# Attention and MoE on one NeuronCore: the first two half sequences attended before any MoE product, reciprocals of those two spread by TensorE, weights loaded in eighths

## The chip, the cores and the metric

The kernel runs on one core of a Trainium2 chip. The metric is the device time of one execution in microseconds (us). A run that lies over 1.5% above the fastest of its kernel counts as slow and stays out of every ratio; the fast runs of one kernel spread over up to 1.5%. Medians and ranges in this text are over all runs of a kernel, the slow ones included. The profile is taken on one execution, and its span is that execution alone.

Engines in the profile: PE is the TensorE matmul, PEld its weight load, DVE VectorE, ACT ScalarE, POOL GpSimd, SP the engine whose queue issues most DMAs. The changed kernel calls its engines through a helper, so that all its lines show one line number (L62); there one reads by tile names. The granted clock is the share of full TensorE speed that the profile records. I call TensorE cold where its matmuls take up to twice as long as the same ones later, and warm otherwise.

## The reference, cut to what matters

Four sequences of 768 tokens, 8 heads of 64. Heads 0, 2 and 6 see everything before them ("retrieval"), the other five see 4 sink keys and a window of 64. The result goes through an MoE-shaped pair of products with a swish between:

```python
scores = scale * np.matmul(q, k.transpose(0, 1, 3, 2))
# ... causal mask for retrieval heads, causal & (sink | window) for the others
a = np.exp(scores)                       # after subtracting the maximum
a = a / (np.sum(a, axis=-1, keepdims=True) + 1e-09)
x = np.matmul(a, v)                      # -> (3072, 512) after putting heads side by side
h = x @ w_in                             # (512, 2048)
g = h * (1.0 / (1.0 + np.exp(-beta * h)))
return g @ w_out                         # (2048, 512)
```

## The kernel before

The work is cut into eight units: half a sequence of 384 queries each. Units 0 and 1 are the two halves of the first sequence. For a unit: load q and k, cast to bf16, transpose on TensorE ("QK"), copies of k for the window blocks ("KX"), scores, exponentials on ACT ("es"), masks on DVE, sums of the exponentials by matmuls, a reciprocal on DVE ("rec"), value products, and a normalizing multiply by the spread reciprocals ("R") that makes xT. Then 16 groups of four first products with w_in (h, tanh on ACT, gT on DVE), and 48 second products with w_out.

The sums of 8 heads stand on 8 partitions for each of 3 blocks of queries, but xT needs each of them on 64 partitions. The kernel writes them to DRAM and reads them back with a broadcast:

```python
        rec = rp.tile([96, 128], F32, name="rec")
        nc.vector.reciprocal(rec, sm[0:96, 0:128])
        rd = dp.tile([8, TU, 128], F32, name="rd")
        for j in range(TU):
            nc.sync.dma_start(out=rd[:, j, :], in_=rec[32 * j:32 * j + 8, :])
        R = rp.tile([128, NP, NQ], F32, name="R")
        src = rd[:]
        for i in range(2):
            nc.sync.dma_start(out=R[i * D:(i + 1) * D], in_=bass.AP(src.tensor, ...))
        # ... in pv(), after the value products of two pairs of heads:
        nc.vector.tensor_mul(x.xT[:, p0:p0 + 2, :], o[:, :, 0:NQ], x.R[:, p0:p0 + 2, :])
```

The identity for the transposes is made in f32 on POOL and cast on DVE, the weights come in quarters, and the order of everything follows from one loop: unit 0's attention, then in each step a piece of the next unit's attention, one first-product group of this unit, and three second products of the last unit.

```python
    ident_f = consts.tile([128, 128], F32, name="ident_f")
    make_identity(nc, ident_f)
    ident = consts.tile([128, 128], BF16, name="ident")
    nc.vector.tensor_copy(out=ident, in_=ident_f)
    # ...
    FS = d_ff // 4
    def load_w_in(s):
        # ... three DMAs for a quarter
        cast(nc.vector, w_in_sb[:, :, s * FS:(s + 1) * FS], f)
    # ...
    for s, f in pieces_a(0):        # the whole attention of unit 0
        f()
    for s in range(4):
        load_w_in(s)
    for s, f in pieces_l(1):        # loads of unit 1
        f()
    for s in range(4):
        load_w_out(s)
    for n in range(N + 1):
        lists = [pieces_a(n + 1), pieces_l(n + 2)]
        for s in range(FO):
            for l in lists:
                for st, f in l:
                    if st == s:
                        f()
            if n < N:
                mm1(units[n], s)
            if n > 0:
                mm2(units[n - 1], s, n == N)
```

The softmax here doesn't subtract the row's maximum and nothing guards it: scores larger than these inputs give would overflow.

Of the kernel before, what the change touches and what calls it, by code (L numbers as in the profile page):

```python
# [15 lines left out]

# [3 lines left out]
SH = [1, 3, 4, 5, 7]  # L20
# [14 lines left out]
def _aff(nc, buf, cm, fstep, base, n):  # L35
    nc.gpsimd.affine_select(
        out=buf,
        in_=buf,
        compare_op=GE,
        fill=0.0,  # L40
        base=base,
        pattern=[[fstep, n]],
        channel_multiplier=cm,
    )


def _view(ap, offset, dims):

    return bass.AP(ap.tensor, ap.offset + offset, [list(ap.ap[0])] + dims)
# [3 lines left out]
def kernel(  # L53
# [13 lines left out]
    nc = tc.nc  # L67
    B, H, S, D = q.shape
    T = S // 128
# [7 lines left out]
    def pool(name, bufs, space=None):  # L77
        kw = {} if space is None else {"space": space}
        return ctx.enter_context(tc.tile_pool(name=name, bufs=bufs, **kw))

    consts = pool("consts", 1)
    stg = pool("stg", 2)
    inp = pool("inp", 2)
    kxp = pool("kxp", 1)
    vp = pool("vp", 2)
    esp = pool("esp", 1)
    xp = pool("xp", 2)
    gp = pool("gp", 2)
    tp_ = pool("tanh", 3)
    op_ = pool("osb", 3)  # L90
    rp = pool("rec", 2)
    dp = pool("dram", 2, bass.MemoryType.DRAM)
    ps_s = pool("ps_s", 2, PSUM)
    ps_m = pool("ps_m", 1, PSUM)
    ps_h = pool("ps_h", 2, PSUM)
    ps_o = pool("ps_o", 1, PSUM)


    def cast(eng, dst, src):
        if eng is nc.scalar:  # L100
            nc.scalar.copy(out=dst, in_=src)
        else:
            eng.tensor_copy(out=dst, in_=src)  # L103

    qk_in = {}
    v_r = {}
    v_s = {}

    def load_qk(b, u, pi):
        ha, hb = PAIRS[pi]  # L110
        res = []
        for nm, src in (("q2", q), ("k2", k)):
            f = stg.tile([128, 2, TU, D], F32, name=nm + "f", bufs=4)
            eng = nc.scalar if (b, u, nm) == (0, 0, "k2") else nc.sync
            eng.dma_start(
                out=f,
                in_=bass.AP(src.tensor, src.offset + ((b * H + ha) * S + u * NQ) * D,
                            [[TU * D, 128], [(hb - ha) * S * D, 2], [1, TU * D]]),
            )
            c = inp.tile([128, TU, 2, D], BF16, name=nm)  # L120
            cast(nc.gpsimd if b > 0 and nm == "q2" else nc.vector, c.rearrange("p t a d -> p a t d"), f)
            res.append(c)
        qk_in[b, u, pi] = res

    def load_v(b, u):

        first_unit = (b, u) == (0, 0)

        def first():
            if u == 0:  # L130
                v_r[b] = vp.tile([128, 3, T, D], BF16, name="vr")
            v_s[b, u] = vp.tile([128, 5, NB[1], D], BF16, name="vs")

        def head(h):
            retr = RETR[h]
            i = (RH if retr else SH).index(h)
            key, step, nb = (u * NQ, 128, TU) if retr else (START[u], STEP[u], NB[u])
            f = stg.tile([128, NB[1], D], F32, name="vf", bufs=8)
            eng = nc.scalar if first_unit and h % 2 else nc.sync
            eng.dma_start(  # L140
                out=f[:, 0:nb, :],
                in_=bass.AP(v.tensor, v.offset + ((b * H + h) * S + key) * D, [[D, 128], [step * D, nb], [1, D]]))
            cast(nc.gpsimd, v_r[b][:, i, u * TU:(u + 1) * TU, :] if retr else v_s[b, u][:, i, 0:nb, :], f[:, 0:nb, :])

        def sinks():
            sk = stg.tile([SINK, H, D], F32, name="sk")
            nc.sync.dma_start(out=sk, in_=v[b, :, 0:SINK, :].rearrange("h p d -> p h d"))
            w0 = 1 if u == 0 else 0
            for i0, n, h, st in ((0, 2, 1, 2), (2, 2, 4, 1), (4, 1, 7, 1)):
                cast(nc.gpsimd, v_s[b, u][0:SINK, i0:i0 + n, w0:NB[u], :],  # L150
                     sk[:, h:h + (n - 1) * st + 1:st, :].unsqueeze(2).to_broadcast([SINK, n, NB[u] - w0, D]))

        return [first] + [lambda h=h: head(h) for h in RH + SH] + [sinks]

    for pi in range(NP):
        load_qk(0, 0, pi)
    for f in load_v(0, 0):
        f()


    ident_f = consts.tile([128, 128], F32, name="ident_f")
    make_identity(nc, ident_f)
    ident = consts.tile([128, 128], BF16, name="ident")
    nc.vector.tensor_copy(out=ident, in_=ident_f)  # L164
    m_f = consts.tile([128, 128], F32, name="m_f")
    nc.gpsimd.memset(m_f, 1.0)
    _aff(nc, m_f, -1, 1, 0, 128)
    mask_c = consts.tile([128, 128], BF16, name="mask_c")
    nc.vector.tensor_copy(out=mask_c, in_=m_f)

    s0_f = consts.tile([128, 128], F32, name="s0_f")
    nc.gpsimd.memset(s0_f, 1.0)
    _aff(nc, s0_f, 1, -1, W - 1, 128)
    nc.gpsimd.memset(s0_f[0:SINK, :], 1.0)
    _aff(nc, s0_f, -1, 1, 0, 128)
    sb_f = consts.tile([128, 60], F32, name="sb_f")
    nc.gpsimd.memset(sb_f, 1.0)
    _aff(nc, sb_f, 1, -1, -(SINK + 1), 60)
    _aff(nc, sb_f, -1, 1, W + SINK, 60)
    nc.gpsimd.memset(sb_f[0:SINK, :], 1.0)  # L180
    mask_s = []
    for u in range(2):
        m = consts.tile([128, NQ], BF16, name=f"mask_s{u}")
        for (blk, off, n) in BLOCKS[u]:
            src = s0_f if (u, blk) == (0, 0) else sb_f
            nc.gpsimd.tensor_copy(out=m[:, off:off + n], in_=src[:, 0:n])
        mask_s.append(m)


    esel = consts.tile([128, 8, 4, 8], BF16, name="esel")  # L190
    nc.gpsimd.memset(esel, 0.0)
    for j in range(8):
        nc.gpsimd.memset(esel[:, j, :, j:j + 1], 1.0)


    QK = []
    for pi in range(NP):
        t = consts.tile([128, 2, S], BF16, name=f"QK{pi}")
        nc.gpsimd.memset(t[:, 1, NQ:NQ + 128], 0.0)
        QK.append(t)  # L200

    beta_h = consts.tile([128, FO], F32, name="beta_h")
    nc.scalar.dma_start(out=beta_h, in_=moe_beta.rearrange("(fo fi) -> fi fo", fi=128))
    nc.vector.tensor_scalar(out=beta_h, in0=beta_h, scalar1=0.5, scalar2=None, op0=MULT)


    w_in_sb = consts.tile([128, NP, d_ff], BF16, name="w_in_sb")
    w_out_sb = consts.tile([128, FO, d_model], BF16, name="w_out_sb")
    FS = d_ff // 4

    def load_w_in(s):
        f = stg.tile([128, 4, FS], F32, name="wf")

        def rows(h, parts, step):
            return bass.AP(moe_w_in.tensor, moe_w_in.offset + h * D * d_ff + s * FS,
                           [[d_ff, parts], [step * D * d_ff, 2], [1, FS]])
        nc.sync.dma_start(out=f[0:D, 0:2, :], in_=rows(0, D, 1))
        nc.sync.dma_start(out=f[D:128, 0:2, :], in_=rows(2, D, 1))
        nc.sync.dma_start(out=f[:, 2:4, :], in_=rows(4, 128, 2))
        cast(nc.vector, w_in_sb[:, :, s * FS:(s + 1) * FS], f)  # L220

    def load_w_out(s):
        f = stg.tile([128, 4, FS], F32, name="wf")
        nc.sync.dma_start(out=f, in_=moe_w_out[s * 512:(s + 1) * 512, :].rearrange("(fo fi) d -> fi fo d", fi=128))
        cast(nc.gpsimd, w_out_sb[:, s * 4:(s + 1) * 4, :], f)


    KXs = {}

    def transpose_pair(x, pi):  # L230
        b, u = x.b, x.u
        c2 = qk_in.pop((b, u, pi))
        if (b, u) == (0, 0):
            ps = ps_h.tile([128, 2, TU, 128], BF16, name="h")
        else:
            ps = ps_m.tile([128, 2, TU, 128], BF16, name="misc")
        for i, c in enumerate(c2):
            for t in range(TU):
                nc.tensor.transpose(ps[:, i, t, :], c[:, t, :, :].rearrange("p a d -> p (a d)"), ident)  # L239
        nc.vector.tensor_copy(  # L240
            out=QK[pi][:, :, u * NQ:(u + 1) * NQ].rearrange("d a (p t) -> d a p t", t=TU),
            in_=ps.rearrange("d a t p -> d a p t"))
        KX = None
        if pi > 0:
            lo = 64 if pi == 3 else 0
            src = QK[pi][lo:128, 1, :]
            KX = kxp.tile([128, NB[u], 128], BF16, name=f"KX{pi}_{u}")
            w0 = 1 if u == 0 else 0
            nc.vector.tensor_copy(out=KX[lo:128], in_=_view(src, START[u], [[STEP[u], NB[u]], [1, 128]]))
# [250 lines left out]
```

## Time and profile before

| | before |
|---|---|
| time, median of the runs beside the changed kernel | 298.12 us (297.81 to 300.03, 4 runs) |
| span of the profiled execution | 293.4 us |
| TensorE busy | 244.4 us, 83% |
| DVE, ACT, POOL busy | 176.2, 131.5, 74.1 us |
| TensorE busy in the first 100 us | 63.3 us |

The table by stretches of the kernel before. After the stretch and its length come busy time and instructions of PE, PEld, DVE, ACT and POOL, then the granted TensorE clock, the DMA share and GB/s.

```profile
0.00:10.00 10.00, 0.00 (x0) 0.10 (x1) 1.35 (x4) 0.00 (x0) 1.18 (x8) 1.00 0.88 196
...
30.00:40.00 10.00, 0.49 (x9) 0.24 (x5) 2.52 (x3) 0.00 (x0) 0.00 (x0) 0.70 0.78 177
40.00:50.00 10.00, 7.12 (x36) 3.16 (x35) 7.97 (x16) 3.38 (x6) 0.69 (x2) 0.62 1.15 279
...
80.00:90.00 10.00, 9.27 (x80) 4.36 (x79) 5.33 (x10) 5.91 (x11) 4.80 (x8) 1.00 1.08 256
...
100.00:290.00 190.00, 181.17 (x1564) 94.41 (x1563) 114.33 (x219) 97.28 (x163) 37.42 (x68) 1.00 0.48 120
```

After 100 us TensorE is busy 181 of 190 us. Before that it does nothing for 10 us, and nearly nothing from 30 to 42. The waits of the kernel before name the releasers (us in total, times, the longest):

```profile
PE h L391 <- DVE xT L383: 13.4, 4, 11.8
...
PE h L239 <- DVE ident L164: 10.5, 1, 10.5
DVE xT L383 <- DMA R<-rd: 9.6, 3, 4.6
```

Two lines of DVE and two of TensorE from the timeline of the kernel before show the first round trip (start, duration, engine, line, operation, and in brackets the idle time before it):

```profile
29.27 0.95 DVE L349 RECIPROCAL rec<-misc 96x128 f32<-96x128 f32 x1 [1.68 <-PE misc L343]
...
41.27 1.82 DVE L383 TENSOR_TENSOR xT<-sp,R 128x768 bf16<-128x768 f32 x2 [4.62 <-DMA R<-rd]
```

```profile
42.28 2.94 PE L391 MATMUL h<-xT,w_in_sb 128*128 128x384 bf16 x8 [11.79 <-DVE xT L383]
45.39 0.50 PE L239 MATMUL misc<-ident,q_437 128*128 128x128 bf16 x3 [0.18 <-DVE q_437 L103]
```

From reciprocal to xT it takes 12.0 us, and TensorE stands idle for 11.79 us. After that its eight first products take 2.94 us, twice the 1.46 us at 65.60, and three transposes 0.50 us against 0.33 at 69.98.

### The profile page before, as it was taken

How to read it: one execution, taken by the hardware profiler on the slowest of the kernel's cores; microseconds unless marked ns; L12 is line 12 of the kernel's file. 1: busy time of each engine (PE TensorE's matmuls, PEld its weight loads, DVE VectorE, ACT ScalarE, POOL GpSimd, SP SyncE). 2: the span in 40 equal slices, each digit the busy share in tenths (PEclk: the TensorE clock that was granted, in tenths of full speed). 3: DMA queues.
4: the chain of work that ended last, by engine and by line, in shares of the span. 5: the costliest groups of instructions: out<-in, count | busy, mean ns of one | idle time of the engine just before them, and what ended most of it. 6: DMA issues, size and time to landing. Idle time of an engine off the chain costs nothing.

```text
span 293.4 us, 5696 instructions
## 1 busy us (share of the span) xinstructions
PE 244.4 (83%) x2196; PEld 128.0 (44%) x2196; DVE 176.2 (60%) x335; ACT 131.5 (45%) x217; POOL 74.1 (25%) x158
## 2 busy tenths in 40 slices
PE   0137129799799989998999979999999999999994
PEld 0124104454345534554455534554455455545541
DVE  1186429985848896627963696449754975353400
ACT  0123006743147529624644487336643684245421
POOL 1291001756342254103460261053000000000000
PEclk9999857999999999999999999999999999999999
DMA  7993699989796799087786879434014110500111
GB/s 217 179 236 101 157 243 275 266 298 330 170 234 183 173 270 264 4 185 198 179 222 153 197 187 224 95 87 143 36 42 106 38 38 8 140 36 36 38 71 71
DMA packets 75850, 44.97 MB, mean 153 GB/s; under 512 B 47984, under 2 KB 68656, under 8 KB 75824
## 3 DMA queue, kind: packets, MB, share of 16 engines
q1 hardware_dynamic: 69536, 43.04, 58.6%
q10 hardware_dynamic: 6288, 1.58, 3.0%
q8 instruction: 17, 0.28, 0.4%
q14 instruction: 9, 0.07, 0.1%
HBM read 38.22 MB, written 6.39 MB: 152 GB/s over the span
## 4 chain that ended last, share of the span: by engine, by line
PE 55%; DVE 18%; DMA 12%; ACT 5%; issue 3%; POOL 3%; SPq 1%; ACTq 0%; DVEq 0%; POOLq 0%
PE h L391 23%; PE o L402 17%; PE sp L382 5%; DMA k2f<-in_k_dram 4%; PE sp L402 4%; DVE gT L395 4%; PE misc L343 3%; DMA wf<-in_moe_w_in_dram 3%; PE sp L309 3%; ACT t L394 3%; DMA R<-rd 2%; DVE QK_214 L240 2%; DMA vf<-in_v_dram 2%; DVE xT L383 2%; POOL vs L103 1%
## 5 line engine op out<-in xcount | busy, mean ns | idle before, releaser
L391 PE MATMUL h<-xT,w_in_sb 128*128 128x384 bf16 x512 | 107.1, 331 | 17.3 <-DVE xT L383 13.4
L394 ACT ACTIVATE t<-h,beta_h 128x384 f32<-128x384 f32 x128 | 74.6, 586 | 104.1 <-PE h L391 102.3
L395 DVE SCALAR_TENSOR_TENSOR gT<-t,h 128x384 bf16<-128x384 f32 x128 | 69.9, 550 | 61.0 <-ACT t L394 60.4
L402 PE MATMUL o<-w_out_sb,gT 128*128 128x512 bf16 x336 | 92.3, 379 | 3.5 <-ACT osb L406 3.4
L391 PEld LDWEIGHTS <-w_in_sb 128*128 128x128 bf16 x512 | 46.1, 98 | 58.2 <-issue 25.4
L402 PEld LDWEIGHTS <-gT 128*128 128x128 bf16 x384 | 36.5, 98 | 37.4 <-issue 6.4
L103 POOL CAST vs<-vf 128x384 bf16<-128x384 f32 (+1 forms) x40 | 22.6, 574 | 47.1 <-DMA vf<-in_v_dram 33.1
L103 POOL CAST vr<-vf 128x192 bf16<-128x192 f32 x24 | 9.1, 386 | 52.2 <-DMA vf<-in_v_dram 51.7
L383 DVE TENSOR_TENSOR xT<-sp,R 128x768 bf16<-128x768 f32 x16 | 14.6, 950 | 10.8 <-DMA R<-rd 9.6
L406 ACT ACTIVATE osb<-o 128x512 f32<-128x512 f32 x21 | 12.5, 594 | 15.2 <-PE o L402 12.7
L103 POOL CAST vs<-sk 4x640 bf16<-4x640 f32 (+3 forms) x24 | 17.3, 745 | 0.0
L343 PEld LDWEIGHTS <-esel 128*32 128x32 bf16 x372 | 9.0, 97 | 7.4 <-issue 7.0
L402 PE MATMUL sp<-w_out_sb,gT 128*128 128x512 bf16 x48 | 10.8, 379 | 0.0
L382 PEld LDWEIGHTS <-vr 128*64 128x64 bf16 x108 | 7.8, 112 | 6.5 <-issue 5.0
L349 DVE RECIPROCAL rec<-misc 96x128 f32<-96x128 f32 x8 | 7.6, 954 | 4.8 <-PE misc L343 4.8
L382 PEld LDWEIGHTS <-vs 128*64 128x64 bf16 x260 | 8.6, 116 | 3.0 <-issue 3.0
L239 PE MATMUL h<-ident,q_104 128*128 128x128 bf16 x3 | 0.5, 298 | 10.5 <-DVE ident L164 10.5
L103 POOL CAST w_out_sb<-wf 128x2048 bf16<-128x2048 f32 x4 | 7.6, 1892 | 5.4 <-DMA wf<-in_moe_w_out_dram 5.4
L309 PE MATMUL sp<-QK_218 64*128 64x384 bf16 (+2 forms) x36 | 8.4, 302 | 0.3 <-ACT es_1_668 L311 0.3
L309 PE MATMUL sp<-QK_212 64*128 64x384 bf16 (+2 forms) x72 | 8.4, 304 | 0.3 <-ACT es_1_556 L311 0.3
L103 DVE CAST w_in_sb<-wf 128x2048 bf16<-128x2048 f32 x4 | 4.8, 1210 | 4.9 <-DMA wf<-in_moe_w_in_dram 4.1
L240 DVE COPY QK_212<-misc 128x768 bf16<-128x768 bf16 x7 | 6.6, 946 | 0.4 <-PE misc L239 0.4
(484 smaller groups left out, 266.7 us busy)
## 6 DMA issues: line engine op xcount, KB each, us to landing
q2f<-in_q_dram SPq DMA_DIRECT2D x32, 192.0 KB
R<-rd SPq DMA_DIRECT2D x16, 384.0 KB
out_dram<-osb SPq DMA_DIRECT2D x24, 256.0 KB
k2f<-in_k_dram SPq DMA_DIRECT2D x28, 192.0 KB
vf<-in_v_dram SPq DMA_DIRECT2D x20, 224.0 KB
wf<-in_moe_w_out_dram SPq DMA_DIRECT2D x4, 1024.0 KB
vf<-in_v_dram SPq DMA_DIRECT2D x16, 192.0 KB
vf<-in_v_dram SPq DMA_DIRECT2D x24, 96.0 KB
```

Source lines behind the costliest of these rows:

```text
L103: eng.tensor_copy(out=dst, in_=src)
L240: nc.vector.tensor_copy(out=QK[pi][:, :, u * NQ:(u + 1) * NQ].rearrange("d a (p t) -> d a p t", t=TU), in_=ps.rearrange("d a t p -> d a p t"))
L309: nc.tensor.matmul(o[j][0], o[j][1], o[j][2], start=True, stop=True)
L343: nc.tensor.matmul(sm[32 * j:32 * j + 32, 0:128], esel[:, hpos, :, :].rearrange("p a b -> p (a b)"), e, start=(done[j] == 0), stop=(done[j ...
L349: nc.vector.reciprocal(rec, sm[0:96, 0:128])
L382: nc.tensor.matmul(a, l, r, start=st, stop=sp)
L383: nc.vector.tensor_mul(x.xT[:, p0:p0 + 2, :], o[:, :, 0:NQ], x.R[:, p0:p0 + 2, :])
L391: nc.tensor.matmul(h[:, 0:NQ], w_in_sb[:, pi, fi * 128:(fi + 1) * 128], x.xT[:, pi, :], start=(pi == 0), stop=(pi == NP - 1))
L394: nc.scalar.activation(out=t, in_=h[:, 0:NQ], func=AF.Tanh, scale=beta_h[:, fi:fi + 1])
L395: nc.vector.scalar_tensor_tensor(out=x.gT[:, fi, :], in0=t, scalar=1.0, in1=h[:, 0:NQ], op0=ADD, op1=MULT)
L402: nc.tensor.matmul(x.o, x.gT[:, fi, ns * 128:(ns + 1) * 128], w_out_sb[:, fi, :], start=(fi == 0), stop=(fi == FO - 1))
L406: nc.scalar.activation(out=osb, in_=x.o, func=AF.Copy, scale=0.5)
```

## The change

The intent has five parts: a shorter start (identity and masks directly in bf16); reciprocals of units 0 and 1 spread by a matmul instead of a DRAM round trip; both attentions first, then their first products (32 groups) back to back, with two-bank PSUM tiles for some of them; weights in eighths, both cast on POOL; and in the steady part attention steps that come earlier, with k casts on POOL and half of the QK copies on ACT. Outputs, transposes, sums and spread reciprocals now share two PSUM banks. The diff also has smaller parts: more staging tiles for the loads, two sets of QK tiles instead of one, and sums taken in turn over the three blocks of queries. The core of the diff (renamings and the helper left out, cuts marked):

```diff
-        R = rp.tile([128, NP, NQ], F32, name="R")
+    def split(x):                      # rec = hi + low part, both bf16
+        hi = rp.tile([96, 128], BF16, name="hi", bufs=1)
+        dve.tensor_copy(out=hi, in_=x.rec)
+        for j in range(TU):
+            r = slice(32 * j, 32 * j + 32)
+            dve.scalar_tensor_tensor(out=hl[r, j * 128:(j + 1) * 128], in0=hi[r], scalar=low[r], in1=x.rec[r],
+                                     op0=MULT, op1=ADD)
+    def spread_pe(x, pi, bank):
+        r = bank()
+        pe.matmul(r[:, 0:NQ], sel[0:96, 2 * pi:2 * pi + 2, :].rearrange("p a d -> p (a d)"), hl[0:96, :],
+                  start=True, stop=True)
+        # ...
+        act.copy(out=x.R[:, pi, :], in_=r[:, 0:NQ])
# ... spread() by DMA stays for units 2 to 7
-    FS = d_ff // 4
+    NS = 8
+    FS = d_ff // NS
# ...
+STEADY = dict(
+    lq=[-34, -33, -32, -31], lv=-30.0, cv=-16.0,
+    T=[-25.5, -24.5, -23.5, -22.5],
+    B={0: [-18, -16, -14], 1: [-20, -18, -16, -14, -12]},
+    S=-9.5, PV=[-4.5, -3.5],
+)
# ... the work is a list sorted by such times; one unit is 16 of them
+            at(t0 - 2, lambda pi=pi: cast_qk(b, u, pi, [pool, pool]))
+            at(t0 + 0.1, lambda pi=pi: qk_copy(x, pi, [act if pi % 2 else dve]))
# ... the start has a table of its own
+    op(-0.5, lambda: act.dma_start(out=beta_h, in_=moe_beta.rearrange("(fo fi) -> fi fo", fi=128)))
+    op(1, lambda: dve.tensor_scalar(out=beta_h, in0=beta_h, scalar1=0.5, scalar2=None, op0=MULT))
+    attn(units[0], 4, 1.5, [dve, act], [dve, act], 14, 8)
+    attn(units[1], 15, 2.2, [dve, pool], [dve], 28, 18.1)
+    for s in range(NS):
+        op(19 + 1.4 * s, lambda s=s: load_w_in(s))
+        op(26 + 1.4 * s, lambda s=s: cast_w_in(s, pool))
+        op(31 + 1.4 * s, lambda s=s: load_w_out(s))
+        op(38 + 1.4 * s, lambda s=s: cast_w_out(s, pool))
+    seq = [(0, 0), (0, 2), (0, 4), (0, 6)]
+    for s in range(0, 8, 2):
+        seq += [(0, s + 8), (1, s)]
+    seq += [(1, s) for s in range(8, 16, 2)]
+    for i, (n, s) in enumerate(seq):
+        op(28.9 + 1.3 * i, lambda n=n, s=s, i=i: mm1_two(n, s, i > 3 and i % 3))
```

## The prediction

> **What bounds it now.** TensorE late, its inputs early. The page gives TensorE 244 of 293.4 us busy. The table by stretches has it busy only 63 of the first 100 us, and 181 of the other 193. Three early gaps: nothing before 10.5 us (transposes wait for an identity made on POOL, copied by DVE); 30 to 42.3 us ("PE h <- DVE xT", 11.8 us), because the reciprocals go to DRAM and back (issued 30.2, xT starts 41.3), after which matmuls run at 320 ns instead of 162 until 47 us, granted clock 0.5; 70 to 84 us, only second products and transposes, because the second unit's reciprocals again take 11 us by DMA. DMA is near saturation to 90 us at 200 to 300 GB/s.
> After 100 us a pair of units takes 62 us. At the warm pace of the timeline (four first-product or three second-product matmuls in 0.65 us) the MoE is 20.8 us a unit; attention I estimate at 5 and 7.2 us for the two halves. So 54 of 62 us is work; the rest is switching latency and DVE-bound stretches (100 to 110 us: DVE 9.5 of 10).
>
> **What the change does.** (1) Identity directly in bf16, masks merged: transposes some 4 us earlier. (2) Reciprocals of units 0 and 1 by four matmuls, four 0.6 us ACT copies and split operations: about 3 us for 11, twice. (3) Both attentions first, then 32 first-product groups back to back: 21 us dense at full clock (ACT needs 32 x 0.586 = 19, so still TensorE-bound). (4) Weights in eighths, cast on POOL. (5) Steady part: k casts leave DVE (4 x 0.35 us a unit), half the QK copies (2 x 0.95) go to ACT: DVE from about 21 to 18 us a unit; reciprocals start earlier.
> Against it: bytes are nearly the same, in the order attention 0, attention 1, w_in, w_out, unit 2, unit 3. By my count at 205 to 300 GB/s the last w_in eighth lands near 44 us, w_out near 58, unit 2's q and k near 65, unit 3's near 75. TensorE's in-order list has unit 3's transposes ahead of unit 2's value products. So I expect first products from 34 to 57 us (first few us cold), then waits for q/k loads until about 77 us around only 10 us of work. What remains at 77 us is about 170 us of warm work; with 10% for switching (12 to 14% now) the span ends near 268 us.
>
> [...]
>
> **Time.** 268 plus the 4.4 us by which the time exceeds the span now: 272 us, 261 to 285. Faster by over 2%: 0.93; within 2%: 0.05; slower: 0.02.
>
> **What would show it.** First transposes at 5 to 7 us; first products at 34 to 57 us, 0.65 us a group once warm; a TensorE dip at 58 to 78 us, its waits leading to q/k loads; DVE below 165 us in total; pairs of units near 58 us.
>
> **What would make it wrong.** Faster loads than I count (no dip: near 260); POOL's 15 us of weight casts, ahead of q/k in its line, delaying unit 2; POOL slowing DVE; new waits on the PSUM banks that outputs, transposes and sums now share.

The sum: about 170 us of warm work left at 77 us, with 10% for switching, ends the span near 268 us, and 4.4 us more make 272. What the trace of before shows of the clock is 0.50 from 35 to 45 us and 1.00 from 50 us.

## The result, and the profile after

| | before | changed |
|---|---|---|
| time, median | 298.12 us (297.81 to 300.03) | 277.19 us (276.27 to 278.61) |
| span of the profiled execution | 293.4 us | 275.4 us |
| TensorE busy | 244.4 us, 83% | 248.1 us, 90% |
| DVE, ACT, POOL busy | 176.2, 131.5, 74.1 us | 159.9, 147.6, 93.5 us |
| TensorE busy in the first 100 us | 63.3 us | 77.5 us |

The ratio is 0.9289, with a 95% interval of 0.9247 to 0.9331. Ratios in this text are the mean time of one kernel's fast runs over the mean of the fast runs of before in the same rounds, so not quite the ratio of the medians quoted. The changed kernel is 7% faster.

The same stretches of the changed kernel:

```profile
0.00:10.00 10.00, 1.64 (x12) 1.12 (x12) 2.27 (x13) 3.32 (x6) 2.87 (x25) 1.00 0.92 198
...
30.00:40.00 10.00, 9.20 (x108) 4.42 (x109) 8.56 (x14) 7.21 (x10) 4.95 (x6) 0.50 0.89 246
40.00:50.00 10.00, 8.93 (x98) 5.43 (x90) 6.38 (x14) 3.80 (x8) 5.85 (x6) 0.74 0.97 289
...
80.00:90.00 10.00, 8.46 (x95) 4.99 (x95) 9.29 (x15) 5.34 (x8) 5.13 (x7) 1.00 0.18 52
...
100.00:290.00 190.00, 170.57 (x1502) 88.48 (x1500) 94.56 (x177) 97.53 (x162) 36.73 (x68) 0.99 0.41 106
```

The hole at 30 to 40 us is filled, at half clock (0.50). Since the span ends at 275.4, the last stretch means 170.6 of 175.4 us. The waits that answer to those shown of before:

```profile
PE sp L62 <- ACT QK L62: 4.8, 1, 4.8
...
DVE xT L62 <- DMA R<-rd: 3.9, 1, 3.9
...
PE h L62 <- DVE gT L62: 1.6, 3, 0.6
```

The long waits of first products (13.4 us) are gone. From the DVE timeline of the changed kernel, the first and second reciprocal are at 23.35 and 42.76 us, and xT begins at 27.07 and 46.65: 3.7 and 3.9 us instead of 12.0 for unit 0, and of 21.5 for unit 1 (61.71 to 83.23 in before).

Where did the 18.0 us of span go? A cut at two fixed points of the work, the start of unit 2's and of unit 7's xT, splits it. The third column is a second profile of the changed kernel (run e8_after_again below), which shows how far two executions of it differ.

| us | before | changed | changed again |
|---|---|---|---|
| start to xT of unit 2 | 107.5 | 98.1 | 100.9 |
| xT of unit 2 to xT of unit 7 | 148.1 | 137.9 | 138.0 |
| xT of unit 7 to the end | 37.7 | 39.4 | 39.5 |

So the front gave 9.4 us (6.6 in the repeat), the steady part 10.2 us, and 1.7 us were given back at the end. The front does not do less by then: 128 first-product matmuls and 66 second ones were done in before at its 107.5 us, 128 and 67 in the changed kernel at 98.1.

### The profile page after: what moved, and what is told of

It is laid out like the page before. It is cut to its first block, busy times and chain, and to the rows that moved or that the text cites. A ratio compares the mean times of both kernels' runs of the same rounds, so it can differ in the third digit from the quotient of the medians.

```text
span 275.4 us, 5756 instructions
## 1 busy us (share of the span) xinstructions
PE 248.1 (90%) x2204; PEld 131.3 (48%) x2204; DVE 159.9 (58%) x314; ACT 147.6 (54%) x246; POOL 93.5 (34%) x175
## 4 chain that ended last, share of the span: by engine, by line
PE 70%; DVE 16%; DMA 6%; ACT 6%; issue 1%; SPq 0%; POOL 0%; ACTq 0%; DVEq 0%
PE o L62 35%; PE h L62 22%; PE sp L62 12%; DVE gT L62 4%; DVE es L62 3%; ACT t L62 3%; DVE KX L62 2%; DMA R<-rd 2%; DVE QK L62 2%; DMA beta_h<-in_moe_beta_dram 2%; DVE xT L62 2%; ACT es L62 1%; DMA k2f<-in_k_dram 1%; ACT QK L62 1%; DVE rec L62 1%
## 5 line engine op out<-in xcount | busy, mean ns | idle before, releaser
L62 PE MATMUL o<-w_out_sb,gT 128*128 128x512 bf16 x384 | 100.9, 380 | 0.1
L62 ACT ACTIVATE es<-sp 128x768 bf16<-128x768 f32 x64 | 49.7, 794 | 18.5 <-PE sp L62 18.3
L62 PE MATMUL sp<-QK 64*128 64x384 bf16 (+2 forms) x108 | 19.4, 330 | 7.0 <-ACT QK L62 4.8
L62 DVE COPY KX<-QK 128x768 bf16<-128x768 bf16 (+7 forms) x48 | 18.7, 393 | 5.5 <-ACT QK L62 4.6
L62 DVE TENSOR_TENSOR es<-es,mask_c 128x256 bf16<-128x256 bf16 (+2 forms) x32 | 14.4, 461 | 12.3 <-ACT es L62 11.2
L62 DVE TENSOR_TENSOR xT<-sp,R 128x768 bf16<-128x768 f32 (+1 forms) x20 | 15.1, 791 | 9.3 <-DMA R<-rd 3.9
L62 DVE COPY QK<-o 128x768 bf16<-128x768 bf16 (+1 forms) x20 | 17.2, 865 | 3.1 <-PE o L62 2.8
L62 POOL CAST k<-k2f 128x384 bf16<-128x384 f32 x28 | 15.0, 537 | 8.1 <-DMA k2f<-in_k_dram 5.0
L62 DVE TENSOR_TENSOR es<-es,mask_s 128x768 bf16<-128x768 bf16 (+1 forms) x24 | 14.3, 602 | 4.5 <-ACT es L62 3.1
L62 POOL CAST vs<-sk 4x1280 bf16<-4x1280 f32 (+3 forms) x16 | 15.8, 1008 | 3.0 <-DMA sk<-in_v_dram 2.6
L62 PE MATMUL sp<-es,vr 128*64 128x384 bf16 (+2 forms) x108 | 16.2, 333 | 0.1
```

The costliest lines, as they stand in the source:

```text
L62: ins = f(*a, **k)
```

## The experiments

All run beside the kernel before. Nine are variants of the changed kernel that undo or alter one or two things, e7 adds one part to the kernel before, e8 is the changed kernel again, and e15 tries to beat both. All gave the reference's result.

### e2_spread_by_dma and e7_before_spread_pe: is it the spreading?

Theory: the reciprocals by TensorE are worth about the round trips that they save. Rival: they are worth nothing alone, because the time is lost elsewhere when the wait goes.

e2 takes that part away from the changed kernel:

```diff
-        op(ts + 0.2, lambda: split(x))
+        op(ts + 0.2, lambda: spread(x))
# ... and instead of four spread_pe and norm_pe:
+        op(ts + 0.55, lambda: norm(x, 0))
+        op(ts + 0.65, lambda: norm(x, 2))
```

> The changed kernel with the reciprocals of units 0 and 1 spread by DMA through DRAM as before, all else kept. Theory A: the value products of unit 0 hold both score buffers in PSUM until the reciprocals are back, 8 to 11 us behind the queued loads, so unit 1's scores start near 38 instead of 30 us and the first products 8 us late: time 5 to 12 us more. Rival B: with unit 1's attention to do meanwhile the round trip is hidden: less than 2 us more.

e7 adds that part alone to the kernel before:

```diff
+        if x.b == 0:
+            # hi and low as in the change, x.R allocated
+            return
         rd = dp.tile([8, TU, 128], F32, name="rd")
# ... and in pv(), before the normalizing multiply:
+                nc.tensor.matmul(h[:, 0:NQ], sel[0:96, ...], hl[0:96, :], start=True, stop=True)
+                nc.scalar.copy(out=x.R[:, pi, :], in_=h[:, 0:NQ])
```

> The kernel before with one part of the change: reciprocals of units 0 and 1 spread by TensorE. Theory A: the spread removes the wait of TensorE from 30 to 42 us and the one before unit 1's first products only down to the arrival of the weights, which are cast at 31, 36 and 45 us in the old load order: 4 to 9 us less (289 to 294). Rival B: most of the gain of the whole change is this one step: 14 us less or more. Rival C: without the new order it brings nothing (within 2 us).

Measured: e2 took 287.62 us (286.55 to 288.19), ratio 0.9641 (0.9587 to 0.9695), 10.4 us over the changed kernel's 277.2. Its front carries it: xT of unit 2 starts at 107.51 us, 9.4 later than in the changed kernel, and from there to xT of unit 7 it takes 139.4 us. The waits of e2 show the old one again:

```profile
PE sp L62 <- DVE xT L62: 13.4, 4, 8.8
...
DVE xT L62 <- DMA R<-rd: 13.3, 5, 3.9
```

e7 took 298.22 us (298.01 to 300.18), ratio 1.0015 (0.9955 to 1.0075): nothing gained. Its xT of units 0 and 1 start 7.7 and 15 us earlier than in before (33.58 and 67.81), yet unit 2's starts at 111.15, later than the 107.54 of before. Three stretches of e7:

```profile
40.00:50.00 10.00, 7.73 (x66) 3.82 (x65) 9.65 (x19) 5.54 (x10) 6.58 (x11) 0.83 1.08 291
50.00:60.00 10.00, 7.00 (x97) 3.46 (x94) 7.49 (x15) 4.84 (x7) 4.99 (x5) 0.75 0.78 277
...
80.00:90.00 10.00, 7.76 (x73) 3.46 (x67) 9.88 (x18) 5.46 (x9) 8.43 (x17) 1.00 0.55 156
```

What follows: the round trip is on the critical path only once the rest of the front is out of the way. Put into the kernel before, the earlier xT runs into a DVE that is busy 9.65 and 9.88 of 10 us in two stretches, and into a granted clock of 0.83 and 0.75 from 40 to 60 us; at 60 us 38 first-product matmuls are done, against 35 in before. The rest of the change without the spreading gives some 10 us (e2 against before), the spreading without the rest nothing, and both together 20 to 21. That DVE is what holds e7 is read from these stretches, not tested.

### e1_beta_pool: the wait for beta at the start

In the changed kernel the first transposes are done by 7.5 us, but the first scores start at 12.29. Its DVE timeline shows why the copies of QK come so late:

```profile
8.56 0.36 DVE L62 CAST q<-q2f 128x384 bf16<-128x384 f32 x1 [0.73 <-DMA q2f<-in_q_dram]
10.46 0.17 DVE L62 TENSOR_SCALAR beta_h<-beta_h 128x16 f32<-128x16 f32 x1 [1.54 <-DMA beta_h<-in_moe_beta_dram]
...
11.18 0.55 DVE L62 COPY QK<-o 128x384 bf16<-128x384 bf16 x1
```

The halving of beta, which nothing needs before the first tanh at 46.9 us, stands in DVE's line before the copies, and DVE sits idle for 1.54 us until it can run. Its DMA, 8 KB behind four loads of k of 192 KB each on the same queue, was issued at 4.03 us and used at 10.46; no run separates the causes of that.

```diff
-    op(1, lambda: dve.tensor_scalar(out=beta_h, ...))
+    op(1, lambda: pool.tensor_scalar(out=beta_h, ...))
```

> The changed kernel with one instruction moved: the scaling of beta (0.17 us) runs on POOL instead of DVE. In the changed kernel it stood in DVE's in-order line before the first QK copy and waited for beta's load until 10.44 us, so the transposes, done by 7 us, were not read before 11.2 us and the first scores came at 12.3. Theory A (the line of the first unit is the bound of the front): first scores near 8 to 9 us, everything up to the first products some 3 us earlier, time 2.5 to 4 us less (274). Theory B (loads of v and of the second unit bound the front): first scores earlier, first products still within 1 us of 45.4, time within 1 us of 277.

Measured: 279.41 us (277.73 to 279.95), ratio 0.936 (0.9304 to 0.9417), so no gain. The wait moved with the instruction, here in POOL's timeline of e1:

```profile
11.44 0.25 POOL L62 TENSOR_SCALAR beta_h<-beta_h 128x16 f32<-128x16 f32 x1 [8.27 <-DMA beta_h<-in_moe_beta_dram]
```

DVE's first QK copy started at 9.96 us instead of 11.18. The first scores came only 1.2 us earlier (11.07), and the mask constants that POOL makes came late instead. xT of units 0 and 1 started at 29.28 and 49.09, not earlier. So e1 moved the wait from one engine's line to another's and does not show what taking it away is worth; that would mean moving the instruction behind what doesn't need it, which was not run.

### e3_dve_steady: is DVE's relief in the steady part worth anything?

```diff
-            at(t0 - 2, lambda pi=pi: cast_qk(b, u, pi, [pool, pool]))
+            at(t0 - 2, lambda pi=pi: cast_qk(b, u, pi, [pool, dve]))
-            at(t0 + 0.1, lambda pi=pi: qk_copy(x, pi, [act if pi % 2 else dve]))
+            at(t0 + 0.1, lambda pi=pi: qk_copy(x, pi, [dve]))
```

> The changed kernel with the DVE work of the steady part as before (k casts and all QK copies on DVE for units 2 to 7, about 3.3 us a unit, 20 us in all). Theory A: TensorE bounds the steady part and DVE has room, time 0 to 3 us more, DVE total near 180 us. Rival B: the relief of DVE is what gained most after 100 us: 6 us more or worse.

Measured: 278.98 us (278.18 to 279.66), ratio 0.9359 (0.9298 to 0.9421). From xT of unit 2 to that of unit 7 it took 137.5 us, against 137.9 and 138.0 in the two profiles of the changed kernel. DVE's busy time rose to 174.6 us (180 expected). So DVE's relief is worth nothing in the steady part.

### e9_old_timing: is it the earlier attention steps?

```diff
-    T=[-25.5, -24.5, -23.5, -22.5],
-    B={0: [-18, -16, -14], 1: [-20, -18, -16, -14, -12]},
-    S=-9.5, PV=[-4.5, -3.5],
+    T=[-16.0, -15.9, -15.0, -14.0],
+    B={0: [-14.9, -13, -10], 1: [-14.9, -13, -12, -10, -9]},
+    S=-7.0, PV=[-3.0, -2.0],
```

(The loads of q, k and v were put back to about their old times, too.)

> The changed kernel with the steps of attention for units 3 to 7 put back to where the kernel before has them against the first products: transposes packed into two steps of the stage just before instead of nine to twelve steps earlier one a step, sums at -7 instead of -9.5, value products at -3. Theory A: the 6 us that the steady part gained come from this spreading in time (e3 showed that DVE's lighter load is not it): 3 to 7 us more. Rival B: from the second bank for the outputs: less than 1.5 us more.

Measured: 280.76 us (279.48 to 282.44), ratio 0.9432 (0.938 to 0.9484), against 277.21 and 0.9322 (0.9264 to 0.938) of the changed kernel in the same call, so 3.5 us more. The stretch from unit 2's to unit 7's xT took 144.5 us instead of 138.0. Of these 6.5 us, 3 come back at the end (36.5 us instead of 39.5), because with the old timing more first and second products are done by unit 7's xT (68 and 97 matmuls are left there, against 76 and 104 in the repeat). So the timing gives 3.5 us of the whole, and it moves 3 more from one stretch of my table to the other. (The profiled spans differ by only 1.2 us, as e9's profiled front was 2.3 us shorter than the repeat's.)

### e8_after_again: how steady is the changed kernel?

> The changed kernel itself, unaltered, as the measure for the other runs of this set on the same chip: 276 to 279 us. How far its front differs from the first trace (first products of both units ending near 71 us, xT of unit 2 at 98 us) tells what a difference of 1 or 2 us between variants is worth.

Measured: 277.21 us (276.49 to 280.08, six runs, all fast), ratio 0.9322 (0.9264 to 0.938). Its profiled run is the slowest of the six, and had the highest clock, 1.0; the five others ran at 0.966 to 0.98 and took 276.49 to 277.73. So the mean clock does not order the times of this kernel, and differences of 1% between two variants are at the edge of what these rounds can tell. Nor does a mean of 1.0 say that TensorE was warm: the repeat's granted clock reads 1.00 in every stretch up to 100 us, yet its transposes were as slow up to 33 us as cold ones elsewhere (0.33 us when warm):

```profile
32.02 0.53 PE L62 MATMUL o<-ident,q 128*128 128x128 bf16 x3
```

### e10_own_banks: the shared PSUM banks

The change lets outputs, transposes, sums and spread reciprocals share two PSUM banks. The prediction feared new waits on them. Here outputs get one bank for themselves and the rest the other.

```diff
-    ps_o = tpool("ps_o", 2, PSUM)
+    ps_o = tpool("ps_o", 1, PSUM)
+    ps_m = tpool("ps_m", 1, PSUM)
# ... transposes, sums and spreads take ps_m
```

> The changed kernel with the PSUM banks of before: one bank for outputs, one for transposes, sums and the spread, instead of two shared by all. Theory A (timing of attention made the steady gain): 0 to 2 us more, mostly the 0.7 us wait for the copy of each output. Rival B (shared pair of banks made it): 4 us more or worse.

Measured: 288.41 us (286.69 to 290.35), ratio 0.9696 (0.963 to 0.9761): 11.2 us more than the changed kernel in the same call. My expectation (0 to 2 us) missed, and rival B's size came without its place: the loss is not in the steady part. The two profiled runs differ by only 6.9 us of span (285.3 against 278.4), so the traces account for that much. The waits of e10:

```profile
PE misc L62 <- DVE hl L62: 4.1, 2, 2.1
...
PE o L62 <- ACT osb L62: 3.8, 6, 0.7
...
PE misc L62 <- DVE QK L62: 3.6, 8, 1.0
```

xT of unit 2 starts at 105.4 (100.9 in the changed kernel's profile of the same call), the steady part is the same (137.1), and the end takes 42.8 instead of 39.5: each output tile there waits about 0.7 us for the last one to leave its only bank. So sharing two banks is right here, not a cost. In before the last unit took its outputs' banks from the scores, so it did not pay that at the end.

### e12_one_first and e14_one_first_warm: the order of the first products

e12 puts the old order back at the start: w_in loaded before unit 1's q and k, and unit 0's first products straight after its attention, mixed with unit 1's attention.

```diff
-    seq = [(0, 0), (0, 2), (0, 4), (0, 6)]
-    for s in range(0, 8, 2):
-        seq += [(0, s + 8), (1, s)]
-    seq += [(1, s) for s in range(8, 16, 2)]
+    seq = [(n, s) for n in range(2) for s in range(0, 16, 2)]
# ... w_in loaded at 4.02, unit 1's q and k at 4.45
-        op(28.9 + 1.3 * i, lambda n=n, s=s, i=i: mm1_two(n, s, i > 3 and i % 3))
+        op(16.1 + 1.6 * i if n == 0 else 28.9 + 1.3 * i, lambda n=n, s=s, i=i: mm1_two(n, s, i > 9 and i % 3))
```

> The changed kernel with the order of before kept at its start: w_in loaded ahead of unit 1's q, k and v, unit 0's first products straight after its attention, then unit 1's attention and first products; all other parts as changed. Theory A (the order is the main gain): first products of unit 0 wait for w_in until 30 us, those of unit 1 end later than 71 us, time 3 to 8 us more. Rival B (with the TensorE spread the order no longer matters, TensorE has the same work in the first 100 us): within 2 us either way.

Measured: 285.77 us in the median, but only one of six runs counts as fast, 277.52 us at a recorded clock of 1.0, the same as the changed kernel. The five others took 282.31 to 289.84 at 0.958 to 0.982. There is no ratio. I don't explain the slow runs; whether their clock was the cause was the question of e14, which adds matmuls of no use so that TensorE stays busy while unit 1 is attended:

```diff
+        if x.b == 0 and u in (1,):
+            for i in range(4):
+                pe.matmul(ps[:, i % 2, 0:NQ], ident, QT[:, u * NQ:u * NQ + NQ], start=True, stop=True)
         for j in range(max(len(o) for o in ops)):   # the scores, into the same bank
```

> The order of e12 (unit 0's first products straight after its attention) with four matmuls of no use before each round of unit 1's scores. Six runs of e12 took 277.5 to 289.8 us, the longer the lower their mean granted clock (1.0 to 0.958). Theory A, that scatter is the clock, lost in the sparse stretch in which unit 1's scores wait for VectorE: with the filler every run has a clock of 0.985 or more and the times are 276 to 281 us, within 3 us of each other. Rival B, the clock is a companion and the order itself is unsteady: the times still scatter over 8 us or more, or all lie above 282 us with a clock near 1.0.

Measured: 283.01 us, five fast runs from 282.16 to 283.05 and one of 286.41, clocks 0.988 to 1.0; ratio 0.95 (0.9453 to 0.9547). Half of Theory A held: with the filler the clock stays up (1.00 from 50 to 70 us, where e12's slow profiled run reads 0.53 and 0.67) and the scatter shrinks from 12 us to 4. The other half missed: no run came near 277. What came is the second form of rival B, all six above 282 us at a clock near 1.0. It does not settle the matter either, because the filler is not free here, as its group of the profile shows:

```profile
L62 PE MATMUL sp<-QK,ident 128*128 128x384 bf16 x40 | 8.2, 328 | 0.0
```

It stands in TensorE's line among products that are needed, so up to 8 us are its own doing. What stays open: whether the order itself is worth anything. The one fast run of e12 says it is worth nothing; its five other runs were slow. The runs don't show more than that the new order was steadier (six of six fast in e8).

### e13_warm: does the cold TensorE cost the front?

In the changed kernel's front TensorE runs at half rate: from 30.70 us three transposes start 0.29 to 0.32 us after the three before them, at 27.09 it is 0.16. From its timeline (three transposes at 15 and at 30.7 us, cold; at 27.09, warm for a while):

```profile
14.97 0.52 PE L62 MATMUL o<-ident,k 128*128 128x128 bf16 x3
...
27.09 0.33 PE L62 MATMUL o<-ident,q 128*128 128x128 bf16 x3
...
30.70 0.50 PE L62 MATMUL o<-ident,q 128*128 128x128 bf16 x3
```

The granted clock does not show all of this: it reads 1.00 up to 25 us, although three transposes take 0.50 to 0.53 us at 4 to 15 us. In before, TensorE was cold after it had stood idle for 11.79 us (2.94 us for the eight matmuls at 42.28, three transposes in 0.50 at 45.39) and warm again at 47.52 (0.35), after 5.2 us with hardly a gap. So e13 tries to keep it warm with work of no use: it puts two dense matmuls before each round of scores in units 0 and 1, as in e14, and four after each group of unit 1's transposes.

> The changed kernel with dense matmuls of no use added while the first two halves are attended: two before each round of scores, into the same bank, overwritten, and four after each group of unit 1's transposes. The reference's result must still come out. In the changed kernel's trace TensorE ran its early matmuls at half rate (three transposes 0.50 to 0.53 us, against 0.33 later) until about 45 us. Theory A, the cold TensorE costs the front: transposes before 40 us come at 0.33 us for three, unit 1's xT is complete by 43 to 45 us instead of 46.7 to 50, first products start at 41 to 42 us, and the time is 274 to 276 us (2 to 3 us less than the changed kernel's 277.2). Rival B, the front goes at the pace of the loads and of VectorE's line: xT of unit 1 stays at 46 to 51 us, the time within 1.5 us of 277.2, perhaps longer, since the added matmuls stand before the scores.

The filler did warm it. The same kinds of line in e13:

```profile
17.25 0.53 PE L62 MATMUL o<-ident,k 128*128 128x128 bf16 x3
...
31.27 0.34 PE L62 MATMUL o<-ident,q 128*128 128x128 bf16 x3
...
34.68 0.33 PE L62 MATMUL o<-ident,k 128*128 128x128 bf16 x3
```

The filler starts at 12.77 us; transposes at 17.25 are still cold, matmuls from 18.3 us warm, until about 38 us. So it was warm 5.5 us after the filler began. Yet the time is 277.16 us (274.64 to 280.03; four of six fast), ratio 0.9283 (0.9226 to 0.934), and xT of unit 1 started at 48.73, inside the rival's window (46 to 51). So the warm stretch, paid for with the filler's own time, brought nothing that can be seen. For that stretch the trace points to DVE. Three lines of e13's DVE timeline:

```profile
30.54 2.15 DVE L62 COPY KX<-QK 128x896 bf16<-128x896 bf16 x2
33.25 0.96 DVE L62 COPY QK<-o 128x768 bf16<-128x768 bf16 x1 [0.56 <-PE o L62]
...
35.48 0.95 DVE L62 COPY QK<-o 128x768 bf16<-128x768 bf16 x1
```

DVE goes from one copy to the next. The pair of KX copies took 2.15 us at 30.54 and 0.82 at 34.42.

But Theory A does not fall with this, because TensorE was cold again before unit 1's attention ended. First a group of 15 matmuls for unit 1's sums in the changed kernel, then in e13 two filler matmuls warm, two cold, and the same group of sums, no faster:

```profile
41.68 1.04 PE L62 MATMUL o<-es,esel 128*32 128x128 bf16 x15
```

```profile
30.57 0.50 PE L62 MATMUL sp<-QK,ident 128*128 128x384 bf16 x2
...
40.49 0.82 PE L62 MATMUL sp<-QK,ident 128*128 128x384 bf16 x2
...
43.74 1.04 PE L62 MATMUL o<-es,esel 128*32 128x128 bf16 x15
```

In the changed kernel TensorE is busy without a gap from 37.0 to 45.4 us, when the first products start, at a granted clock of 0.5, and from 40 to 45 us DVE is busy only 2.58 of 5 us. At full clock that stretch could be up to 4 us shorter (an estimate from the granted 0.5: half of its 8.4 us). In e13 TensorE was busy without a gap from 38.7 to 45.6 us, at the cold durations above, part of it with filler. So e13 did not test the stretch in which a cold TensorE is most likely to cost time; that stays open.

### e4_quarters: the weights in eighths

```diff
-    NS = 8
+    NS = 4
# ... staging tiles bufs=4 -> bufs=2, and the table's steps 1.4 -> 2.8
```

> The changed kernel with the weights in quarters again, two staging tiles instead of four of half the size, casts on GpSimd as in the change. Theory A, eighths matter little because both weight matrices have landed before TensorE needs them or within a few us: 277 to 279 us. Rival B, with quarters the first w_in block is usable about 2.5 us later and each cast takes twice as long, so first products wait: first products start 2 to 4 us later than 45.4, and the time is 280 to 282 us.

Measured: 278.46 us (277.14 to 280.16), ratio 0.9363 (0.9316 to 0.9411). Both expectations hold in part. First products start at 50.07 us, 4.6 and 3.1 later than in the two profiles of the changed kernel (45.44, 46.96), and the waits of e4 name the load of w_in:

```profile
POOL w_in_sb L62 <- DMA wf<-in_moe_w_in_dram: 11.3, 4, 6.6
```

But the time is only 1.2 to 2.2 us more by the ratios (0.9322 and 0.9289 for the changed kernel), with overlapping intervals, and xT of unit 2 starts at 99.50, between the two profiles. Eighths make the first products early, and little of it reaches the end.

### e15_wide_and_act: an attempt to beat both

```diff
-        op(28.9 + 1.3 * i, lambda n=n, s=s, i=i: mm1_two(n, s, i > 3 and i % 3))
+        op(28.9 + 1.3 * i, lambda n=n, s=s, i=i: mm1_two(n, s, i > 1 and i % 3))
-            at(base + p["cv"] + 5.6 + 0.7 * j, lambda sk=sk: cast_sink(b, u, *sk, pool))
+            at(base + p["cv"] + 5.6 + 0.7 * j, lambda sk=sk: cast_sink(b, u, *sk, act))
```

The second edit answers two lines of the changed kernel, of DVE and of POOL:

```profile
83.02 1.76 DVE L62 TENSOR_TENSOR es<-es,mask_c 128x256 bf16<-128x256 bf16 x1
```

```profile
82.95 2.24 POOL L62 CAST vs<-sk 4x1792 bf16<-4x1792 f32 x2
```

The same mask takes 0.28 us at 78.55. Of the 16 masks of this form in the changed kernel two take over 1.7 us, 1.76 at 83.02 and 1.73 at 182.68, and both run beside such casts on POOL; no other takes over 0.83. That the casts slow them is my inference; the traces show only that they coincide.

> Two small changes of the changed kernel, to try to beat it: two-bank tiles are used for first products from the third pair on instead of the fifth (in its trace the first four pairs took 2 us each, for two banks only), and the casts of the sink rows of v go to ScalarE instead of GpSimd (a mask on VectorE took 1.76 us instead of 0.28 next to such a cast). Theory A, both waits are paid: first products end about 1.5 us earlier, some 0.3 us a unit are saved in the steady part, 274 to 276 us. Rival B, both are hidden by other waits: 277 us within 1 us; ScalarE's added work (six units of about 1 us) might cost up to 2 us.

Measured: 278.35 us (276.60 to 283.11, five of six fast), ratio 0.933 (0.9274 to 0.9385). Rival B: first products are slightly ahead at 60 us (72 matmuls instead of 68; the repeat of the changed kernel had 53), and the masks of that form took at most 0.63 us (a mean of 0.35, against 0.55 and 0.50 in the two profiles of the changed kernel). Nothing of it arrives. No version beat the changed kernel beyond the uncertainty.

## Why the prediction was right, point by point

The time was predicted at 272 us (261 to 285) and measured at 277.19, and the class (faster, at 0.93) was right.

- **"TensorE late, its inputs early" and the three gaps.** Right. The front gave 9.4 us of the 18.0 us of span, and the stretches show the gap at 30 to 42 us gone.
- **(1) "transposes some 4 us earlier", first at 5 to 7 us.** They started at 4.15, against 10.50. But the scores started at 12.29, against 18.09, and the path then led through the beta wait in DVE's line, which I had not seen. What that wait costs stays open: e1 only moved it to POOL.
- **(2) "about 3 us for 11, twice".** 3.7 and 3.9 us, for 12.0 and 21.5. e2 shows its worth in place: 10.4 us. e7 shows that it has none in the kernel before. The prediction counted the parts as a sum; the runs show that this part needs the others.
- **(3) First products "from 34 to 57 us".** This step failed. They ran from 45.4 to 71.4 us. The start was 11 us late, because unit 1's attention ended at 45 us; the prediction had a cold TensorE only in the first few us of the first products. What made the attention late stays open. Two candidates are read from the trace: DVE's line (8.56 of 10 us busy from 30 to 40), not tested alone, and a TensorE busy at half clock (0.50) from 37.0 to 45.4, which e13 did not keep warm. The length was 26 us instead of 23, since each of the first four pairs took about 2 us with only two PSUM banks (TensorE waits 0.48 to 0.58 us for gT three times from 48 to 52 us); e15 shows that relief of that does not reach the end.
- **Loads: "waits for q/k loads until about 77 us".** Wrong in place, since the first products came later: most of step (3)'s delay fell into time in which I had TensorE waiting for loads, so two errors offset each other, by luck. When unit 2's q and k had landed (60 to 64 us), TensorE still had first products to do. The dip came at 80 to 90 us (8.46 of 10 busy), smaller, and with DVE at 9.29 of 10.
- **"What remains at 77 us is about 170 us of warm work; with 10% for switching", span 268.** Counted from the trace, 384 first-product matmuls at 0.163 us (four in 0.65), 368 second ones at 0.217 (three in 0.65) and six attentions of 6.1 us (my estimate in the prediction) remain at 77 us: about 179 us at most. It took 198.4, that is 11% more. (My own sum is loose: 77 plus 170 plus 10% is 264, and 268 has 12% in it.) So switching was right, and the work left at 77 us was mis-sized by 9 us, by step (3). The span became 275.4, 7.4 more than I had.
- **"plus the 4.4 us by which the time exceeds the span".** Wrong by 2.7. I had set the median of three runs against a span from another execution. In every run that reports both, of the kernel before too, the difference is 1.7 to 1.8 us, and up to 2.1 in e4. This took back a third of the error of the front, by luck.
- **(4) Eighths.** 1 to 2 us (e4), not clearly separable from zero.
- **(5) DVE "from about 21 to 18 us a unit", below 165 in total; pairs near 58 us.** Right: 159.9 us in total, and from reciprocal to reciprocal (units 3 to 7) a pair takes 57.4 us, against 61.7. But the cause is not DVE's relief: e3 undid it and lost nothing in the steady part. e9 shows 3.5 us of it to be the earlier attention steps. What is left of the 10.2 us (3.7, after the 6.5 that e9 takes back in that stretch) no run assigns; e10 rules out the shared banks (137.1 us in that stretch), and deeper staging, a second set of QK tiles and the order of the sums are candidates that I didn't test.
- **"POOL slowing DVE", "new waits on the PSUM banks".** The first is seen on single instructions beside POOL casts (1.76 us for 0.28), without a cost that e15 could find. The second did not come: e10 shows the sharing to be better than a split.

## What to carry to other kernels

A wait of 11 us on the critical path can be worth nothing when removed alone and 10 us once the neighbouring limits are gone, so test a part both ways: taken from the new kernel and added to the old one. A busy engine is not thereby the limit: DVE's load in the steady part looked costly, and putting it back changed nothing there (e3). Before an experiment is said to clear a suspect, check in its trace that it removed the suspect where it matters: e13's filler warmed TensorE up to 38 us, and the stretch that ends in the first products, 37 to 45 us, stayed cold. Place an instruction by when its input lands and its result is needed: the scaling of beta kept its engine idle until its load had landed, DVE for 1.54 us in the changed kernel and POOL for 8.27 in e1, with needed work behind it.
